# A memory-attention and two-layer MoE kernel: its first stage as 390 one-engine parts in a fixed order

## The chip, the cores and the metric

The kernel runs on one core of a Trainium2 chip. The metric is the device time of one execution in microseconds. The engines are TensorE (PE, with its weight loads as PEld), VectorE (DVE), ScalarE (ACT), GpSimd (POOL) and SyncE (SP), whose queue issues the loads and stores.

## The reference

Batch 4, 8 heads, 576 tokens, head size 64, 32 memory slots; the MoE layers have 512 to 1536 and back. The inputs are 64-bit floats; the kernel reads attention inputs as 32-bit floats and decodes weights from their two 32-bit halves.

```
a = exp(phi - max(phi, axis=2)); a = a / (sum(a, axis=2) + 1e-09)
k_m = einsum('bhsm,bhsd->bhmd', a, k)
v_m = einsum('bhsm,bhsd->bhmd', a, v)
scores = q @ k_m.T / sqrt(64)
attn = exp(scores - max); attn = attn / (sum(attn) + 1e-09)
x = (attn @ v_m), tokens by (heads x 64)
x = ((x @ w_a) * (x @ w_b)) @ w_out
g = x @ w_gate
out = (g * sigmoid(g) * (x @ w_val)) @ w_out2
```

## The kernel before

The work has three stages. The first is the attention of the four batches, together with the first two of the twelve column blocks (f = 0, 1) of the first MoE layer. The second stage is column blocks 2 to 11 of that layer, in five rounds of two. The third is the second layer. Matmuls that need more precision are made from a high and a low part: the high part is a ScalarE copy, the low part is the difference, on VectorE or GpSimd (`split`).

For each batch b the attention goes like this. `phi` is loaded; its maximum goes over the nine rows a partition holds (`over_r`, tiles `rm`, `pm`), then over partitions by TensorE (`mx`) and VectorE (`nmx`); `phi` is shifted and exponentiated. TensorE contracts it with k and v (`kv`, 144 instructions), its sum (`es`, on GpSimd) gives `rs`, which scales `kv` into `kvm`; TensorE transposes that (`kvT`) into `kb` and `vt`. `q` is transposed (`qT`). The scores come in two calls (`sc`, 40 instructions each: twice 16 and 4), each followed on VectorE by `mx`, a subtraction, ScalarE's exponential, `den` and a multiplication. The transposed result is `aT`, split high and low.

The first MoE layer never forms x @ w. `vw` is v_m times a weight block; `s1a` and `s1b` are the two products of `aT` with it (two products of 12 matmuls for each batch and block), `bs` their product, split into `gh` and `gl`; `s2` multiplies by `w_out` (`oh`, `ol`), in four parts of 12 matmuls for a batch and a pair of blocks, added into `acc`.

A weight chunk is 128 x 512. It is loaded (`raw`, four buffers, at most three chunks ahead), ScalarE and VectorE reshape its bits (`dec_a`, lines 123 to 134: three VectorE operations), GpSimd adds the two halves (lines 148, 150), and `w_out` chunks are split (172, 176). A chunk is 512 KB, a `phi` 576 KB, a half of k or v 576 KB, a `q` 1024 and 128 KB. All loads go through SyncE's queue in order. `q` of the last batch uses the slot of the third batch's transposed `q`, k and v of it use slots of batches 0 and 1.

The first stage is written by hand as a string, `PLAN`: a letter for a whole step of a batch (`0a`), `T` for the next weight chunk with all its operations, `V` for the next `vw` and `D` for the next step of `first_dense`. The framework's scheduler takes this order as a priority and issues each engine's instructions in an order of its own, by its estimates of time; it also mixes work of the second stage into the first. The first loads are in a string of their own, `LOADS`. The second and third stage have lists of their own (`BLOCK`, and the loops at the end).

All TensorE results go to `bank2` tiles: four buffers of two PSUM banks.

Of the kernel before, what the change touches and what calls it, by code (L numbers as in the profile page):

```python
# [18 lines left out]
def kernel(  # L19
# [75 lines left out]
    raw, dec, whl, ohl = {}, {}, {}, {}  # L95
# [24 lines left out]
    def chunk_bits(c):  # L120
        hi, lo = raw[c][:, :, 1], raw[c][:, :, 0]
        a = dec_p.tile([128, 512], I32, tag="a", name="dec_a")
        nc.scalar.activation(out=f32(a), in_=f32(hi), func=ACTF.Abs)
        nc.vector.tensor_scalar(  # L124
            out=f32(a), in0=f32(a), scalar1=LEAST, scalar2=MOST, op0=ALU.max, op1=ALU.min
        )
        nc.scalar.activation(  # L127
            out=lo, in_=lo.bitcast(U32), func=ACTF.Copy, scale=2.0 ** -29
        )
# [7 lines left out]
        dec[c] = a  # L137

    def chunk_round(c):
        a = dec.pop(c) if whole(c) else dec[c]  # L140
        lo = raw.pop(c)[:, :, 0]
        if whole(c):
            i, j = c
            if j == 0:
# [3 lines left out]
            nc.gpsimd.tensor_tensor(out=o, in0=ai, in1=li, op=ALU.add)  # L148
        else:
            nc.gpsimd.tensor_tensor(out=a, in0=a, in1=lo, op=ALU.add)  # L150

    def whole(c):

        return c[0] < NF and c[1] < 2

    def chunk_dst(c):
        i, j = c
        if j < 2:
            return [x[:, :, j, :] for x in whl[i]]
        return ohl[i]  # L160

    def chunk_src(c):
        a = f32(dec[c])
        return a.rearrange("p (k f) -> p k f", k=KD) if c[1] < 2 else a

    def chunk_hi(c):
        i, j = c
        if j == 0:
            whl[i] = [w_p.tile([128, KD, 2, 128], FP32R, tag="w", name=f"w{x}") for x in "hl"]
        elif j == 2:  # L170
            ohl[i] = [w_p.tile([128, DM], FP32R, tag=f"o{x}", name=f"o{x}") for x in "hl"]
# [9 lines left out]
    def ticks_to(n):  # L181
        while ticks[0] < n:
            t = ticks[0]
            for step in (chunk_bits, chunk_round, chunk_hi, chunk_lo):
                if step in (chunk_bits, chunk_round) or not whole(order[t]):
                    step(order[t])
# [49 lines left out]
    mx_t, et_t, kvm_t, qT_t, sc_t = {}, {}, {}, {}, {}  # L236
# [9 lines left out]
    def att_pre(b):  # L246

        m = at_p.tile([128, PR, M], FP32, tag="pm", name="pm")
        over_r(eng("rmx", b), m, phi_t[b], ALU.max)
        mx_t[b] = m  # L250

    def att_phi(b):

        pt = bank2("mx")
        nc.tensor.transpose(
            pt[:, 0, 0:128], mx_t.pop(b).rearrange("p j m -> p (j m)"), ident
        )
# [4 lines left out]
        )  # L262
        for g in range(2):
# [4 lines left out]
        m = pt[:, 1, 0:128]  # L268
        if eng("sub", b) is nc.gpsimd:
            m = at_p.tile([128, 128], FP32, tag="nm", bufs=1, name="nm")  # L270
            nc.scalar.copy(out=m, in_=pt[:, 1, 0:128])
        et_t[b] = m

    def att_norm(b):
        x = phi_t[b]
        m = et_t.pop(b).rearrange("p (j o m) -> p j o m", j=PR, o=1)
        eng("sub", b).tensor_tensor(
            out=x, in0=x, in1=m.to_broadcast([128, PR, R, M]), op=ALU.add
        )
        nc.scalar.activation(out=x, in_=x, func=ACTF.Exp)  # L280

    def att_kv(b):


        x = phi_t.pop(b)
        es = at_p.tile([128, PR, M], FP32, tag="es", bufs=1, name="es")
        over_r(eng("sum", b), es, x, ALU.add)
        pkv = bank2("kv")
        for r in range(R):
            for j in range(PR):  # L290
                for g in range(2):
# [8 lines left out]
                    )  # L300
        sm = pkv[:, 0, 2 * D:2 * D + 2]
        nc.tensor.matmul(
            sm, lhsT=es.rearrange("p j m -> p (j m)"), rhs=ones, start=True, stop=True
        )
        rs = sm_p.tile([128, 2], FP32, tag="rs", name="rs")
        nc.vector.tensor_scalar(out=rs, in0=sm, scalar1=1e-9, scalar2=None, op0=ALU.add)
        nc.vector.reciprocal(out=rs, in_=rs)
        kv = at_p.tile([128, 3, 2, D], FP32, tag="kvm", name="kvm")
        for g in range(2):
# [3 lines left out]
            )  # L313
            nc.vector.tensor_scalar(
# [3 lines left out]
        kvm_t[b] = kv  # L318
        if b + 2 < B:
            load_phi(b + 2)  # L320

    def att_blocks(b):


        kv = kvm_t.pop(b)
        pT = bank2("kvT")
        for i in range(3):
            nc.tensor.transpose(
                pT[:, 0, 128 * i:128 * i + 128], kv[:, i].rearrange("c o d -> c (o d)"), ident
            )  # L330
        kT = pT[:, 0, 0:256].rearrange("c (g j m) -> c g j m", g=2, j=PR)
        for o in range(2):
            rows = slice(D * o, D * o + D)
            nc.scalar.copy(out=kb[b % 2][rows, :, :, o], in_=kT[rows])
        nc.scalar.copy(out=vt[b], in_=pT[:, 0, 256:384])

    def att_q(b, c):


        if c == 0:  # L340
            qT_t[b] = slot(ld_slots[b][0], [128, PR * R // 2, 128], FP32, f"qT{b}")
            kv_t.pop((b, 0))
# [10 lines left out]
    def att_scores(b, t):  # L353

        if t == 0:
            sc_t[b] = at_p.tile([128, R, PR, M], FP32, tag="sc", name="sc")
        pc = bank2("sc")
        for o in range(2):
            j = 2 * t + o
            for r in range(0, R, 2):  # L360
                for g in range(2):
# [10 lines left out]
                    else:  # L372
# [31 lines left out]
    def att_out(b, c):  # L404

        if c == 0:
            aT[b] = slot(ld_slots[b][1], [128, 2, 2, S], FP32R, f"aT{b}")
            kv_t.pop((b, 1))
# [11 lines left out]
        split(  # L420
            dst[0], dst[1],
            pa[:, 0:n * 128].rearrange("c (r g p) -> c r g p", g=2, p=P),
        )

    def att_stage(b, s):

        {
            "a": lambda: att_pre(b), "b": lambda: att_phi(b), "c": lambda: att_norm(b),
            "d": lambda: att_kv(b), "e": lambda: att_blocks(b),
            "f": lambda: att_q(b, 0), "g": lambda: att_q(b, 1), "h": lambda: att_q(b, 2),  # L430
            "i": lambda: att_scores(b, 0), "j": lambda: att_scores(b, 1),
            "k": lambda: att_softmax(b, 0), "l": lambda: att_softmax(b, 1),
            "m": lambda: att_out(b, 0), "n": lambda: att_out(b, 1),
        }[s]()
# [215 lines left out]
    for _ in dense:  # L650
        pass
# [141 lines left out]
```

## Time and profile before

| | |
|---|---|
| median of 3 runs | 923.0 us (921.26 to 924.1) |
| profiled execution | 921.33 us, its span 919.5 us |
| TensorE (PE) busy | 861.4 us, 94% |
| VectorE (DVE) busy | 513.5 us, 56% |
| ScalarE (ACT) busy | 317.8 us, 35% |
| GpSimd (POOL) busy | 210.2 us, 23% |
| mean granted TensorE clock | 0.971 |

The span reaches from the first to the last instruction. A clock of 1.0 is TensorE's upper level, 2.4 GHz, 0.5 the lower, 1.2 GHz; a value between is a mean over a stretch. Busy matmuls overlap, so the durations of single ones add up to more than the time they take. In rows of the trace, L12 is a line of the kernel, "s" is the tile `s2` or `s4`, and PE matmuls in the trace count the passes of a 32-bit matmul one by one.

### The profile page before, as it was taken

The numbers are of one execution on the slowest core, as the hardware profiler recorded it, in microseconds if no ns is written. First come the engines' busy times: TensorE is split into PE (matmuls) and PEld (weight loads), VectorE is DVE, ScalarE is ACT, GpSimd is POOL, SyncE is SP. The second block draws the span as 40 slices with busy tenths as digits, with TensorE's granted clock in tenths as the row PEclk, the third lists the DMA queues.
The fourth block names the chain that finished last, engine by engine and source line by source line (L and its number), as shares of the span: only waits on it lengthen the run. The fifth ranks groups of instructions, "written<-read, shape, count | busy, mean of one in ns | idle before, by whom it ended". The sixth has DMA issues, their size and how long they took to land.

```text
span 919.5 us, 16206 instructions
## 1 busy us (share of the span) xinstructions
PE 861.4 (94%) x7068; PEld 799.8 (87%) x7068; DVE 513.5 (56%) x714; ACT 317.8 (35%) x502; POOL 210.2 (23%) x165
## 2 busy tenths in 40 slices
PE   3685897899999999999999999999999999999997
PEld 2574786789989989999999999999999999999995
DVE  3698637654765745649736316544554753644343
ACT  2465434542523424235424433312421420411210
POOL 2253013331422314315004203211220420410000
PEclk9687997999999999999999999999999999999999
DMA  9972104120211300202002201110210200000027
GB/s 330 375 240 92 53 3 138 47 92 1 92 47 47 112 4 24 70 1 92 1 1 69 70 1 46 46 47 1 92 47 1 91 25 1 1 1 1 1 46 160
DMA packets 42439, 60.02 MB, mean 65 GB/s; under 512 B 4224, under 2 KB 30848, under 8 KB 42368
## 3 DMA queue, kind: packets, MB, share of 16 engines
q1 hardware_dynamic: 42368, 58.99, 20.4%
q8 instruction: 55, 0.90, 0.4%
q14 instruction: 16, 0.13, 0.0%
HBM read 54.26 MB, written 4.72 MB: 64 GB/s over the span
## 4 chain that ended last, share of the span: by engine, by line
PE 71%; issue 10%; DVE 7%; DMA 6%; POOL 2%; SPq 2%; ACT 2%; POOLq 0%; ACTq 0%; DVEq 0%
PE s L460 27%; PE val L468 17%; PE gate L468 17%; PE s1b L468 5%; PE s1a L468 4%; DMA raw<-in_moe_w_b_dram 2%; DVE dec_a L124 2%; PE vw L481 2%; DMA q<-in_q_dram 2%; DVE dec_a L130 1%; DVE dec_a L134 1%; DMA raw<-in_moe_w_a_dram 1%; DMA raw<-in_moe_w_out_dram 1%; DVE gl L78 1%; DVE vwl L78 1%
## 5 line engine op out<-in xcount | busy, mean ns | idle before, releaser
L460 PE MATMUL s<-oh,g 128*128 128x512 f32 x432 | 137.0, 390 | 0.0
L460 PE MATMUL s<-gh,oh 128*128 128x288 f32 x384 | 114.6, 301 | 3.4 <-ACT gh L77 2.2
L460 PE MATMUL s<-gl,oh 128*128 128x288 f32 x384 | 113.2, 295 | 1.5 <-DVE gl L78 0.9
L460 PE MATMUL s<-gh,ol 128*128 128x288 f32 x384 | 112.9, 295 | 0.0
L698 DVE TENSOR_TENSOR sg<-gate,sg 128x576 f32<-128x576 f32 x48 | 36.3, 756 | 107.3 <-ACT sg L697 107.3
L460 PEld LDWEIGHTS s<-oh,g 128*128 128x128 f32 x432 | 81.1, 188 | 16.4
L176 POOL TENSOR_TENSOR wl<-dec_a,wh 128x512 fp32r<-128x512 f32 x24 | 36.3, 1536 | 250.4 <-ACT wh L172 244.7
L150 POOL TENSOR_TENSOR dec_a<-dec_a,raw 128x512 int32<-128x512 int32 x48 | 64.2, 1338 | 98.2 <-issue 44.2
L127 ACT ACTIVATE raw<-raw 128x512 int32<-128x512 uint32 x72 | 48.9, 680 | 107.4 <-DMA raw<-in_moe_w_out_dram 42.1
L460 PE MATMUL s<-ol,g 128*128 128x512 f32 x216 | 84.1, 389 | 0.0
L468 PE MATMUL gate<-x2l,wh 128*128 128x288 f32 x384 | 82.4, 296 | 0.0
L468 PE MATMUL val<-x2l,wh 128*128 128x288 f32 x384 | 82.2, 296 | 0.0
L468 PE MATMUL val<-x2h,wh 128*128 128x288 f32 x384 | 82.2, 296 | 0.0
L468 PE MATMUL val<-x2h,wl 128*128 128x288 f32 x384 | 82.2, 296 | 0.0
L559 DVE TENSOR_TENSOR acc<-s,acc 128x576 f32<-128x576 f32 x80 | 59.5, 751 | 40.5 <-PE s L460 40.4
L468 PE MATMUL gate<-x2h,wl 128*128 128x288 f32 x384 | 82.0, 295 | 0.0
L468 PE MATMUL gate<-x2h,wh 128*128 128x288 f32 x384 | 82.0, 295 | 0.0
L468 PE MATMUL s1b<-aT,vwh 128*128 128x288 f32 x384 | 75.8, 316 | 5.2 <-DVE aT L78 2.4
L460 PEld LDWEIGHTS s<-gh,oh 128*128 128x128 f32 x384 | 71.9, 188 | 6.6 <-ACT gh L77 3.0
L725 DVE TENSOR_TENSOR oacc<-s,oacc 128x1024 f32<-128x1024 f32 (+1 forms) x50 | 55.7, 1115 | 34.2 <-PE s L460 33.2
L460 PEld LDWEIGHTS s<-gl,oh 128*128 128x128 f32 x384 | 72.2, 188 | 2.0 <-DVE gl L78 1.2
L697 ACT ACTIVATE sg<-gate 128x576 f32<-128x576 f32 x48 | 31.2, 649 | 122.8 <-PE gate L468 122.8
(97 smaller groups left out, 1721.8 us busy)
## 6 DMA issues: line engine op xcount, KB each, us to landing
raw<-in_moe_w_out_dram SPq DMA_DIRECT2D x24, 512.0 KB, 3.4
raw<-in_moe_w_a_dram SPq DMA_DIRECT2D x12, 512.0 KB, 4.9
raw<-in_moe_w_b_dram SPq DMA_DIRECT2D x12, 512.0 KB, 3.6
raw<-in_moe_w_gate_dram SPq DMA_DIRECT2D x12, 512.0 KB, 3.5
raw<-in_moe_w_val_dram SPq DMA_DIRECT2D x12, 512.0 KB, 3.5
kv<-in_k_dram SPq DMA_DIRECT2D x8, 576.0 KB, 9.7
kv<-in_v_dram SPq DMA_DIRECT2D x8, 576.0 KB, 9.7
out_dram<-oacc SPq DMA_DIRECT2D x36, 128.0 KB, 2.4
```

The source lines that it names most:

```text
L78: (eng or nc.vector).tensor_tensor(out=lo, in0=src, in1=f32(hi), op=ALU.subtract)
L124: nc.vector.tensor_scalar(out=f32(a), in0=f32(a), scalar1=LEAST, scalar2=MOST, op0=ALU.max, op1=ALU.min)
L127: nc.scalar.activation(out=lo, in_=lo.bitcast(U32), func=ACTF.Copy, scale=2.0 ** -29)
L150: nc.gpsimd.tensor_tensor(out=a, in0=a, in1=lo, op=ALU.add)
L176: nc.gpsimd.tensor_tensor(out=lo, in0=chunk_src(c), in1=f32(hi), op=ALU.subtract)
L460: nc.tensor.matmul(dst, lhsT=l, rhs=r, start=(i == 0), stop=(i == n - 1))
L468: nc.tensor.matmul(p[:, hb, 0:HB], l, x, start=(i == 0), stop=(i == n - 1))
L481: nc.tensor.matmul(pv[M * j:M * j + M, g, n], lhsT=vt[b][rows, M * j:M * j + M], rhs=whl[f][0][rows, j].rearrange("p t c -> p (t c)"), sta ...
L559: nc.vector.tensor_tensor(out=acc[b][:, dt], in0=pv, in1=acc[b][:, dt], op=ALU.add)
L697: nc.scalar.activation(out=t, in_=pg, func=ACTF.Sigmoid)
L698: nc.vector.tensor_tensor(out=t, in0=pg, in1=t, op=ALU.mult)
L725: nc.vector.tensor_tensor(out=dst, in0=p[:, 0:n], in1=dst, op=ALU.add)
```

## The change

The steps of the first stage become generators that hand back after each group of instructions of one engine. `PLAN` becomes a list of 390 such parts: a name begins a piece of work when it first stands there, and each later time goes on to the next part of the same piece. `p` is `phi` to `kvT` and `kb` of a batch, `e` the sum, `q` the `qT`, `s` a score call with its softmax, `o` the `aT`, `a` and `b` the two products of `s1`, `d` a part of `s2`, `c` a weight chunk (by number), `v` a `vw`; capitals are loads (`P` phi, `K` and `L` halves of k and v, `Q` q, `W` a weight chunk). Afterwards each instruction of the list is tied behind the one before it on its engine, and each later instruction behind the engine's last of the list. These ties need no semaphore. The second and third stages' lists stay as they are.

```
-    def chunk_bits(c):
+    def chunk(c):
+        i, j = c
         hi, lo = raw[c][:, :, 1], raw[c][:, :, 0]
         a = dec_p.tile([128, 512], I32, tag="a", name="dec_a")
         nc.scalar.activation(out=f32(a), in_=f32(hi), func=ACTF.Abs)
+        yield
+        nc.scalar.activation(
+            out=lo, in_=lo.bitcast(U32), func=ACTF.Copy, scale=2.0 ** -29
+        )
+        yield
         nc.vector.tensor_scalar(
...
     PLAN = """
-    0a 0b 0c 0d T 1a 0f 0g 0e 0h 1b T 0i 1c 0k 0j 0l T 1d 0m T V 0n V 1e
...
+    P0 W1 L0 K0 W0 Q0 p0 P1 W3 c1 p0 c1 p0 p0 c1 K1 p0 c1 c1 c1 c1 p0 e0 L1 p0 Q1 c0 c0 c0 W2 c0
+    c0 c0 c0 p0 q0.1 p0 p0 q0.0 q0.1 W4 q0.2 q0.0 p0 p1 p0 q0.2 W5 c3 p0 p0 p0 p1 c3 s0.0 p1 c3
...
-    LOADS = "p0 k0 w0 l0 q0 w1 p1 w2 k1 l1 q1 k2 l2 q2"
...
+    begun = {}
     for op in PLAN.split():
...
+        if op not in begun:
+            begun[op] = work(op)
+        next(begun[op], None)
+    ticks[0] = sum(op[0] == "c" for op in begun)
+    n_vw[0] = sum(op[0] == "v" for op in begun)
...
+    def behind(ins, in_turn):
+        for x in ins:
+            if x.engine in engines and not isinstance(x, mybir.BassTilePoolBoundary):
+                if x.engine in last:
+                    tc.add_manual_dep(x, last[x.engine], no_sync, reason="order of the plan")
+                if in_turn:
+                    last[x.engine] = x.name
+
+    planned = list(nc.cur_bb.bb.instructions)
+    behind(planned, True)
...
     for _ in pend:
         pass
+    behind(list(nc.cur_bb.bb.instructions)[len(planned):], False)
```

Three pieces of the engines' orders follow, each before and then after. A row is a line of the program, the operation, and the tiles it writes and reads; numbers behind a name tell buffers apart.

The first piece is VectorE after the first batch's `phi` is shifted. Before, `rm` and `pm` are those of the second batch, `dec_a` rows belong to two weight chunks, and `rs` and `kvm` to the first batch:

```order
L241 TENSOR_TENSOR rm<-phi 128x384
L134 SCALAR_TENSOR_TENSOR dec_a<-raw,dec_a 128x512
L242 TENSOR_TENSOR rm<-rm,phi 128x384
L243 TENSOR_TENSOR rm<-rm 128x4x32
L244 TENSOR_TENSOR pm<-rm 128x128
L124 TENSOR_SCALAR dec_a<-dec_a 128x512
L130 TENSOR_SCALAR dec_a<-dec_a 128x512
L134 SCALAR_TENSOR_TENSOR dec_a<-raw,dec_a 128x512
L306 TENSOR_SCALAR rs<-kv 128x2
L307 RECIPROCAL rs<-rs 128x2
L314 TENSOR_SCALAR kvm<-kv,rs 128x64 x2
```

After, at the same place, the chunk is number 0:

```order
L134 TENSOR_SCALAR dec_a<-dec_a 128x512
L137 TENSOR_SCALAR dec_a<-dec_a 128x512
L141 SCALAR_TENSOR_TENSOR dec_a<-raw,dec_a 128x512
L287 TENSOR_SCALAR rs<-kv 128x2
L288 RECIPROCAL rs<-rs 128x2
L422 COPY qT_247<-qT 128x1024
L298 TENSOR_SCALAR kvm<-kv,rs 128x64 x2
L231 TENSOR_TENSOR rm<-phi 128x384
L232 TENSOR_TENSOR rm<-rm,phi 128x384
L233 TENSOR_TENSOR rm<-rm 128x4x32
```

The second batch's `rm` has moved from ahead of the first batch's `rs` to behind its `kvm`, and one chunk stands ahead of `rs` where parts of two stood.

The second piece is TensorE between `s2` and the next `s1`, in the middle of the stage. Before, `aT` is that of the third batch, the `s` rows are `s2` of the second, `kv` that of the fourth:

```order
L460 MATMUL s_1134<-gl,oh 128x288
L460 MATMUL s_1134<-gh,ol 128x288
L255 MATMUL mx<-ident,pm 128x128
L481 MATMUL vw<-w,vt_95 32x256 x16
L264 MATMUL mx<-ident,nmx 64x128 x2
L412 MATMUL aT<-ident,sc 128x128 x9
L468 MATMUL s1b<-aT_1190,vwh 128x288
L293 MATMUL kv<-kv_370,phi 32x128 x4
L293 MATMUL kv<-kv_723,phi 32x128 x4
```

After, `aT` and `s1b` are the second batch's; the `kv` sum just ended is the fourth's, `kvT` and the scores are the third's:

```order
L282 MATMUL kv<-ones,es 128x2
L307 MATMUL kvT<-ident,kvm 128x128 x3
L397 MATMUL aT<-ident,sc 128x128 x5
L350 MATMUL sc<-kb_97,qT_805 64x64 x8
L360 MATMUL sc<-kb_97,qT_805 64x32 x2
L350 MATMUL sc<-kb_97,qT_805 64x64 x8
L360 MATMUL sc<-kb_97,qT_805 64x32 x2
L350 MATMUL sc<-kb_97,qT_805 64x64 x8
L360 MATMUL sc<-kb_97,qT_805 64x32 x2
L350 MATMUL sc<-kb_97,qT_805 64x64 x8
L360 MATMUL sc<-kb_97,qT_805 64x32 x2
L435 MATMUL s1b<-aT_953,vwh 128x288 x4
```

Before, a batch's `aT` is followed by its own `s1`, and the next batch's scores come after that; now the next batch's scores stand between a batch's `aT` and its `s1`, and the batch after that has its `kv` done too.

The third piece is SyncE's queue around the last batch's `q`. Before, k and v of the last batch's second half, then `q`:

```order
L223 DMA kv_723<-in_k_dram 128x2x576
L223 DMA kv_723<-in_v_dram 128x2x576
L110 DMA raw<-in_moe_w_b_dram 128x4x256
L110 DMA raw<-in_moe_w_a_dram 128x4x256
L110 DMA raw<-in_moe_w_b_dram 128x4x256
L230 DMA q_1122<-in_q_dram 128x4x512
L230 DMA q_1122<-in_q_dram 128x4x64
```

After:

```order
L110 DMA raw<-in_moe_w_b_dram 128x4x256 x3
L213 DMA kv_756<-in_k_dram 128x2x576
L213 DMA kv_756<-in_v_dram 128x2x576
L110 DMA raw<-in_moe_w_a_dram 128x4x256 x2
L220 DMA q_1128<-in_q_dram 128x4x512
L220 DMA q_1128<-in_q_dram 128x4x64
L115 DMA raw<-in_moe_w_out_dram 128x1024
```

Three weight loads now stand ahead of the last batch's k and v, and two between them and `q`; two of these five chunks (12 and 13) belong to the second stage.

## Rows read from the trace of the kernel before

**Rows 1.** Windows: busy us of each engine (instructions), then PEclk, DMA share, GB/s.

```profile
0.00:200.00 200.00, 149.52 (x1845) 128.08 (x1846) 133.51 (x216) 93.87 (x159) 60.16 (x57) 0.87 0.47 157
84.00:147.00 63.00, 54.40 (x790) 46.84 (x789) 35.88 (x63) 23.96 (x44) 9.47 (x11) 0.93 0.11 33
200.00:459.10 259.10, 257.62 (x2279) 243.54 (x2279) 162.42 (x220) 100.69 (x155) 70.85 (x51) 1.00 0.14 44
```

**Rows 2.** Chain that ended last, second stage and start of third: start, us, what.

```profile
342.64 1.02 PE vw L481 x32
...
348.66 1.60 PE s1a L468 x12
...
459.11 3.20 PE gate L468 x24
```

**Rows 3.** Groups by line and shape, PE, 0 to 200 us: busy, mean ns, idle before.

```profile
L468 PE MATMUL s1b<-aT,vwh 128*128 128x288 f32 x104 | 25.2, 357 | 4.1 <-DVE aT L78 2.4 <-DVE bs L522 1.2 <-ACT aT L77 0.3
L460 PE MATMUL s<-gh,oh 128*128 128x288 f32 x76 | 23.2, 316 | 3.4 <-ACT gh L77 2.2 <-ACT acc L455 0.8 <-DVE vwl L78 0.4
...
L481 PE MATMUL vw<-w,vt 64*32 64x256 f32 x261 | 10.5, 414 | 1.8 <-POOL w L148 1.8
```

**Rows 4.** Timeline of DVE, first 26 us: start, us, what, idle before and releaser.

```profile
6.21 0.29 DVE L243 TENSOR_TENSOR rm<-rm 128x128 f32<-128x128 f32 x1
...
10.23 0.43 DVE L124 TENSOR_SCALAR dec_a<-dec_a 128x512 f32<-128x512 f32 x1 [0.33 <-ACT dec_a L123]
...
20.68 0.56 DVE L241 TENSOR_TENSOR rm<-phi 128x384 f32<-128x384 f32 x1 [1.68 <-DMA phi<-in_phi_dram]
...
22.34 1.27 DVE L243 TENSOR_TENSOR rm<-rm 128x128 f32<-128x128 f32 x1
...
25.38 0.15 DVE L306 TENSOR_SCALAR rs<-kv 128x2 f32<-128x2 f32 x1
```

**Rows 5.** Timeline of PE, 0 to 50 us, three starts after a wait.

```profile
26.24 0.47 PE L328 MATMUL kvT<-ident,kvm 128*128 128x128 f32 x1 [7.39 <-ACT kvm L310]
...
40.83 1.30 PE L412 MATMUL aT<-ident,sc 128*128 128x128 f32 x5 [2.20 <-DVE rs L306]
...
49.45 0.61 PE L468 MATMUL s1b<-aT,vwh 128*128 128x288 f32 x1 [1.14 <-DVE aT L78]
```

**Rows 6.** Groups by line and shape, DVE, 0 to 200 us.

```profile
L124 DVE TENSOR_SCALAR dec_a<-dec_a 128x512 f32<-128x512 f32 x25 | 20.2, 813 | 17.1 <-ACT dec_a L123 17.1
L134 DVE SCALAR_TENSOR_TENSOR dec_a<-raw,dec_a 128x512 int32<-128x512 int32 x25 | 20.2, 809 | 0.4
L130 DVE TENSOR_SCALAR dec_a<-dec_a 128x512 int32<-128x512 int32 x25 | 14.7, 589 | 0.3
L522 DVE TENSOR_TENSOR bs<-s1a,bs 128x576 f32<-128x576 f32 x12 | 9.0, 751 | 7.2 <-PE s1a L468 7.2
...
L78 DVE TENSOR_TENSOR vwl<-vw,vwh 128x1024 fp32r<-128x1024 f32 x4 | 4.9, 1220 | 4.8 <-ACT vwh L77 4.8
```

**Rows 7.** Timeline of PE, 90 to 109 us, full clock.

```profile
90.72 1.73 PE L293 MATMUL kv<-kv,phi 64*32 64x128 f32 x102
...
98.68 1.04 PE L347 MATMUL qT<-ident,q 128*128 128x128 f32 x8
...
106.54 0.69 PE L364 MATMUL sc<-kb,qT 128*64 128x64 f32 x16
...
108.01 0.30 PE L374 MATMUL sc<-kb,qT 64*64 64x32 f32 x4
```

**Rows 8.** Waits of PE, 0 to 300 us: total, times, longest.

```profile
PE aT L412 <- DVE sc L400: 17.4, 3, 8.8
```

**Rows 9.** Timeline of POOL at the held-up `rm`.

```profile
21.97 1.49 POOL L148 TENSOR_TENSOR w<-dec_a,raw 128x512 int32<-128x512 int32 x1 [5.82 <-DMA raw<-in_moe_w_a_dram]
```

**Rows 10.** Timeline of SP's queue: the last batch's `q`.

```profile
108.39 0.92 SPq L230 DMA_DIRECT2D q<-in_q_dram  x2
```

**Rows 11.** The tile `q`: its loads, issue to landing.

```profile
DMA to landing us min/median/max: 5.1/11.5/13.9
```

More of the change, by code (lines that the diff above doesn't have):

```diff
@@ L94 @@
     at = {c: n for n, c in enumerate(order)}
-    raw, dec, whl, ohl = {}, {}, {}, {}
+    raw, whl, ohl = {}, {}, {}
     def ready(i, j):
@@ L118, in chunk_load, with whole @@
         raw[c] = t
-    def chunk_bits(c):
+    def whole(c):
+        return c[0] < NF and c[1] < 2
+    def chunk(c):
+        i, j = c
         hi, lo = raw[c][:, :, 1], raw[c][:, :, 0]
@@ L183, in ticks_to @@
             t = ticks[0]
-            for step in (chunk_bits, chunk_round, chunk_hi, chunk_lo):
-                if step in (chunk_bits, chunk_round) or not whole(order[t]):
-                    step(order[t])
+            for _ in chunk(order[t]):
+                pass
             if t + AHEAD < len(order):
@@ L262, in att_phi @@
         )
+        yield
         for g in range(2):
@@ L267, in att_phi @@
             )
[L268 to L277, printed above, removed]
+        yield
+        m = pt[:, 1, 0:128].rearrange("p (j o m) -> p j o m", j=PR, o=1)
+        nc.vector.tensor_tensor(
             out=x, in0=x, in1=m.to_broadcast([128, PR, R, M]), op=ALU.add
         )
+        yield
         nc.scalar.activation(out=x, in_=x, func=ACTF.Exp)
[L282 to L287, printed above, removed]
+        yield
         pkv = bank2("kv")
@@ L313, in att_kv @@
             )
+        yield
+        for g in range(2):
             nc.vector.tensor_scalar(
@@ L520, in emit_s1, with s2_part @@
         yield
-        pa = prod(0, "s1a")
-        nc.vector.tensor_tensor(out=bs, in0=pa, in1=bs, op=ALU.mult)
+        nc.vector.tensor_tensor(out=bs, in0=pa_t.pop((b, f)), in1=bs, op=ALU.mult)
+        yield
+        vw_t.pop((b, f))
         g = [g_p.tile([128, 2, HB], FP32R, tag=f"g{x}", name=f"g{x}") for x in "hl"]
-        split(
-            g[0], g[1], bs,
-            eng("gl", 2 * b + f) if f < 2 else nc.gpsimd if f % 2 == 0 else nc.vector,
-        )
+        nc.scalar.copy(out=g[0], in_=bs)
+        yield
+        e = eng("gl", 2 * b + f) if f < 2 else nc.gpsimd if f % 2 == 0 else nc.vector
+        e.tensor_tensor(out=g[1], in0=bs, in1=f32(g[0]), op=ALU.subtract)
         g_t[b, f] = g
         yield
+    def emit_s1(b, f):
+        x = s1_b(b, f)
+        for n in range(2):
+            next(x)
+        yield
+        for _ in s1_a(b, f):
+            pass
+        for _ in x:
+            pass
+        yield
     acc, x2 = {}, {}
-    def emit_s2(b, idx):
+    def s2_part(b, idx, dt):
         first, last = idx[0] == 0, idx[-1] == NF - 1
-        if first:
+        if first and b not in acc:
             acc[b] = slot(ld_slots[b][2], [128, KD, 2, HB], FP32, f"acc{b}")
-        if last:
+        if last and b not in x2:
             x2[b] = [
@@ L634, with work @@
+    def work(op):
+        w, n = op[0], [int(x) for x in op[1:].split(".")]
+        return {
+            "p": att_phi, "e": att_sum, "q": att_q, "s": att_scores, "o": att_out,
+            "a": s1_a, "b": s1_b,
+            "c": lambda n: chunk(order[n]), "v": lambda n: vw_part(vws[n]),
+            "d": lambda b, dt: s2_part(b, (0, 1), dt),
+        }.get(w, lambda *n: load(w, *n))(*n)
     make_identity(nc, ident)
@@ L638 @@
         nc.vector.memset(ones[P * g:P * g + P, g:g + 1], 1.0)
-    dense = first_dense()
+    begun = {}
     for op in PLAN.split():
-        if op == "D":
-            next(dense, None)
-        elif op == "V":
-            next_vw()
-        elif op == "T":
-            ticks_to(min(ticks[0] + 1, before(4, 0)))
-        else:
-            att_stage(int(op[0]), op[1])
-    for _ in dense:
-        pass
+        if op not in begun:
[3 more added lines that the diff above has]
+    n_vw[0] = sum(op[0] == "v" for op in begun)
+    for b in range(B):
+        for f in range(2):
+            g_t.pop((b, f))
+    no_sync = mybir.DependencyInfo(
+        mybir.DependencyClass.NoSync, mybir.DependencyReason.DATA
+    )
+    engines = {e.engine for e in (nc.tensor, nc.vector, nc.scalar, nc.gpsimd, nc.sync)}
+    last = {}
+    def behind(ins, in_turn):
[7 more added lines that the diff above has]
+    behind(planned, True)
     s1, s2 = s1_parts(), s2_parts()
```

276 lines of the change are left out of this document (134 added, 142 removed).

## Prediction

> **What bounds the kernel now.** I read the windows first, because one number for the whole span hides everything here. From 200 us to 459.1 us TensorE is busy 257.62 of 259.10 us at full clock; in the first 200 us it is busy 149.52 us, and at a mean granted clock of 0.87 [rows 1]. So the second and third stages are bound by TensorE, the change doesn't touch their lists, and only the first stage has time to give.
>
> How much? I value what TensorE had done by 200 us at the prices of a full stretch: a product of 12 matmuls (`s1a`, `s1b`) takes 1.60 us, one part of `s2` is 12 matmuls of the same size, and a pair of `vw` parts takes 1.02 us [rows 2]. By 200 us it had issued 104 `vwh` matmuls of `s1b` (8 a product: 13 products, and the `s1a` that goes with each), 76 `gh,oh` matmuls of `s2` (4 a part: 19 parts) and 261 of `vw` (16 a part: 16.3 parts) [rows 3]. The first stage as the new list draws it needs 8, 8, 16 and 10 of these. The surplus is second-stage work: 10 products (16.0 us), 3 `s2` parts (4.8) and 6.3 `vw` parts (3.2), together 24.0 us. Without it the first stage would have ended at about 176 us.
>
> A second way to the same point: the first `gate` matmul starts at 459.11 [rows 2]. The second stage has five blocks, each of 16 products, 16 `s2` parts and 8 `vw` parts, 25.6 + 25.6 + 4.1 = 55.3 us; less the part `v8` that the list has already, 276 to 277 us in all. I allow 9 us for its own losses: about 6 is what separates 259.1 us after 200 from the 253 us of work then left, and 3 is an estimate for a ragged start. 459.1 - 277 - 9 = 173 us. I use this form below, since both kernels share it:
>
> span = T1 + 277 + 9 + (919.5 - 459.1 = 460.4), with T1 the end of the first stage on TensorE; before, T1 is 173.
>
> **What the change does, and its first milestone.** No arithmetic is added; the ties lie between instructions of one engine, which keeps its order anyway, so I cost them at nothing. What moves is which instruction an in-order engine has in front of it.
>
> Before, VectorE has the four `rm` operations of the second batch and two weight chunks ahead of `rs`. The first of these waits for its load until 20.68, `rs` runs at 25.38 [rows 4], and TensorE, done with `kv` early, idles 7.39 us before `kvT` at 26.24 [rows 5]. In the new order `rs` stands behind chunk 0 alone, and `rm` comes after `kvm` (first piece of the order above). The data for `kv` comes as before, since the same 3.5 MB are ahead of it. Chunk 0's load is the seventh instead of the eighth; with its three VectorE operations done by 17, `rs` is out at 17.2, one `qT` copy stands between, `kvm` is done at about 20.1, and `kvT` starts 6 us earlier than before.
>
> From `kvT` to the first `aT` transposes it took 40.83 - 26.24 = 14.6 us [rows 5]; the new order has one weight chunk and one `vwl` more in this chain, so I take 15.5 and get 35.6. From there to an unbroken `s1` before took 49.45 - 40.83 = 8.6 us [rows 5]. Now VectorE has `rs`, one chunk (0.81 + 0.59 + 0.81 = 2.2 us [rows 6]), `kvm` and both `aT` differences in front: 0.3 + 2.2 + 0.6 + 1.5 = 4.6 us. First `s1` at about 40.5, 9 us earlier.
>
> **The rest of the first stage.** TensorE's whole list at full clock: 16 products and 16 `s2` parts 51.2 us; 10 `vw` parts 5.1; 576 `kv` matmuls at 1.73/102 us, 9.8; 72 `qT`, 36 `aT` and 12 `kvT` transposes at 1.04/8 us, 15.6; 8 score calls at 108.31 - 106.54 = 1.77 us, 14.2 [rows 7]; some 3 us of small ones. Sum 99 us. Two batches of `kv` and scores, one and a half of `qT` and one `aT` are done at 40.5, 16 us; 83 are left, so TensorE can't end before 123.
>
> VectorE: 133.51 us busy in the first 200 us [rows 1]. Off that list are 13 of the 25 chunks (13 x 2.2 = 28.7), 4 of 12 `bs` (3.0), 3 of 4 wide `vwl` (3.7) [rows 6] and some five `acc` and `gl` of the same size as `bs` (3.8): 94.3 us are left. Adding up the new order's rows, some 25 of them are done at 35.6, so VectorE could end at 105, and behind its last difference TensorE has at most eight `s2` parts, 12.8 us: 118. The two engines are nearly level, so neither alone sets the end; handing over does.
>
> For that I use the middle batches before. From 84 to 147 us TensorE did two batches in 63 us, idle for 8.6 and at clock 0.93, worth 4.4 [rows 1]: 6.5 us lost for each batch, mostly in `aT` waiting for the softmax of its own batch, 17.4 us in three waits [rows 8]. The new order puts `s2` of the batch before, `kv` and scores of the next batch between those (second piece), so part of it is filled. Three batches are left: 19.5 us if nothing is filled, 0 if all is. I take 13, nearer the upper end, because an order that cannot move meets delays of its own and four two-bank PSUM tiles let TensorE run ahead little. T1 = 123 + 13 = 136.
>
> The loads cost nothing by this sum. Those of the third batch now stand behind a wait for the first batch's scores, which end at about 30 us in this walk, when the 12 MB asked for ahead of them are still landing until about 40: the loads up to the second `phi`, 5.8 MB, took until 20.68 [rows 4], 0.3 MB a us.
>
> Sum: 136 + 277 + 9 + 460.4 = 882.4 us of span, against 919.5. The profiled run took 921.33 us, 1.8 above its span, and the median of the runs shown is 1.7 above that. I predict **886 us**, 37 less.
>
> **Two rules of the Trainium skill.** An order that can't move pays for every late input with all that stands behind it; the row for that is VectorE's 1.68 us wait for a load at 20.68, with `rs` behind it, for which TensorE lost 7.39 [rows 4, 5]. The Trainium skill, "TensorE: Matmul & The Clock Gate", table of specifications, says that the queues of ScalarE, VectorE and GpSimdE are strict FIFO; the trace agrees. By that rule the change could as well make such waits as remove them, which is the slower rival's ground.
>
> A VectorE operation can also be held up by GpSimd: `rm` L243 takes 0.29 us at 6.21 with GpSimd idle and 1.27 us at 22.34, while GpSimd adds from 21.97 on [rows 4, 9]. The Trainium skill, "SBUF — State Buffer", section on the shared port pair, says this is an exclusive lock in which the loser fully blocks; the trace agrees, the long one ends just after GpSimd does. The rival it makes is worked out next.
>
> **Rivals.**
> *All handovers filled.* T1 = 123, span 869.4, time 873. For it: VectorE and TensorE are level and every batch has another's work beside it. Against: TensorE restarts at half clock at 40 us, and the losses never were zero in any batch before.
> *VectorE held up by GpSimd.* The first stage has some 38 us of GpSimd work (12 chunks at about 1.3 us, splits and sums), which now lies in 100 us instead of 170. The first operation of a chunk takes 0.43 us undisturbed, as at 10.23, and 0.81 in the mean [rows 4, 6]; if the other two lose as much together, 0.76 a chunk or 9 us of 12 chunks, about a quarter of GpSimd's time, is in my sum already. If all of it blocked, 28 us more fall on VectorE: 118 + 28 = 146, with half to all of the 13 us of handovers 152 to 159; time 902 to 909. Half as dense, it gives about 895.
> *Slower: the fourth batch's `q` comes late.* It is 1.1 MB that waits on the SyncE queue for the third batch's scores (their slot), and now also stands behind two weight loads that wait for GpSimd to free `raw` buffers (third piece). Before, it was issued at 108.39, and a `q` load takes 5.1 us at the least to land [rows 10, 11]. In my walk the scores end near 74 and those buffers come free at about the same time. What follows `qT` of the fourth batch is 45 us of TensorE, with some 8 of handovers, so T1 is the issue time + 58. From an issue at 118 us on, T1 is above 176 and the kernel slower; at 125 the time is about 933. For it: three waits in one queue; against: it needs a slip of over 40 us.
> *No change.* The old order was the scheduler's own, the new one moves the same work; if both wait for the same chains, T1 stays at about 173 and the time at 923. Against: TensorE lost over 70 of 200 us, and `rs` and `aT` show where.
>
> **Chances.** Forecast (876 to 895) 0.58; handovers filled (below 876) 0.12; VectorE held up (895 to 915) 0.20; no change 0.03; slower 0.07. The time is that of the first, 886. The range 870 to 906 takes in T1 from 123 to 156: most of the second case and three quarters of the third. About 0.3% (2.8 us) is what a measurement of this kernel tells from no change: faster 0.90, same 0.03, slower 0.07.
>
> **What would show it.** Right: `kvT` of the first batch near 20 us and the first `s1` near 41; TensorE's first second-stage product near 136; second stage and third as long as before (277 + 9 and 460); clock 1.0 from 50 us on. Wrong, and how: VectorE's chunk operations well over 2.2 us a chunk (held up); a TensorE wait for a `q` or `kv` load after 50 us (the loads' order); a T1 near 136 with a longer second stage, because it starts with 12 decoded chunks where before had 25 decoded at 200 us [rows 6]. That last one would break the sum at a place where I assumed that nothing changes.

## The result, and the profile after

The changed kernel took 885.63 us (median of 4 runs, 884.45 to 888.8), the kernel before 922.39 beside it: ratio 0.9605, 95% interval 0.9575 to 0.9636. The profiled execution took 884.45 us, span 882.7, mean granted clock 0.994 (before 0.971). 886 us were predicted, but that the sum came out is luck, through two errors of equal size: the first stage ended 14 us earlier than I put it, and the second stage took 14 us longer.

The windows show both. Columns as in [rows 1]; the cuts are the first unbroken `s1`, the end of the first stage (T1), 200 us, the first `gate`, and the last matmul.

```profile
0.00:40.50 40.50, 22.75 (x478) 18.36 (x479) 27.10 (x59) 19.13 (x34) 12.06 (x18) 1.00 1.01 348
40.50:122.30 81.80, 79.52 (x1120) 72.79 (x1126) 62.38 (x107) 46.91 (x82) 26.75 (x23) 1.00 0.41 135
122.30:200.00 77.70, 71.34 (x642) 65.63 (x643) 59.08 (x76) 38.19 (x60) 30.14 (x21) 0.96 0.28 88
200.00:422.20 222.20, 215.48 (x1890) 202.81 (x1890) 147.64 (x196) 90.89 (x139) 65.07 (x46) 1.00 0.15 49
422.20:876.40 454.20, 454.20 (x2953) 428.22 (x2951) 217.10 (x277) 123.30 (x188) 79.40 (x57) 1.00 0.12 36
```

In the second line TensorE (first busy column) is idle for 2.3 of 81.8 us at full clock, where before it lost 6.5 us a batch. In the third and fourth, the second stage, it is idle 6.4 and 6.7 us, 13 in all; before it was idle for 1.5 us from 200 us to the first `gate` [rows 1].

TensorE's timeline has the milestones. Columns: start, us, engine, line, operation, count, and in brackets the idle time before it and what ended it.

```profile
20.49 0.62 PE L307 MATMUL kvT<-ident,kvm 128*128 128x128 f32 x3 [0.31 <-DVE qT L422]
33.60 1.17 PE L397 MATMUL aT<-ident,sc 128*128 128x128 f32 x9 [0.43 <-DVE rs L287]
...
38.42 0.80 PE L435 MATMUL s1a<-aT,vwh 128*128 128x288 f32 x4
...
122.20 1.09 PE L448 MATMUL vw<-w,vt 64*32 64x256 f32 x32
...
142.23 0.61 PE L427 MATMUL s<-gh,oh 128*128 128x288 f32 x1 [4.31 <-DVE bs L493]
...
226.07 0.79 PE L435 MATMUL s1a<-aT,vwh 128*128 128x288 f32 x4 [1.48 <-DVE acc L543]
...
422.06 0.42 PE L435 MATMUL gate<-x2h,wh 128*128 128x288 f32 x2
```

The starts that answer to [rows 5] came at 20.5, 33.6 and 38.4 us. The `vw` at 122.20 stands right behind the last `s2` part of the first stage, so T1 is 122.2. The first `gate` is at 422.1: the second stage took 299.9 us. TensorE's three largest waits in it (total, times, longest):

```profile
PE s1a L435 <- DVE acc L543: 4.7, 4, 1.5
PE s L427 <- DVE bs L493: 4.3, 1, 4.3
PE s L427 <- DVE vwl L470: 2.0, 3, 1.1
```

One long stall stands at its start, at 142 us, after which TensorE ran at half clock (0.66 and 0.50 in the windows 140 to 144 and 144 to 148 us); four shorter ones, up to 1.5 us, stand at the turns of its rounds. VectorE is named in these rows; 2.0 us more fell to ScalarE (`gh`, `bs`). What VectorE did, by the groups of a weight chunk's three operations (count, busy, mean ns), first up to T1 and then from 122 to 171 us, where the second round begins:

```profile
L141 DVE SCALAR_TENSOR_TENSOR dec_a<-raw,dec_a 128x512 int32<-128x512 int32 x12 | 8.3, 693 | 0.4
L137 DVE TENSOR_SCALAR dec_a<-dec_a 128x512 int32<-128x512 int32 x12 | 6.2, 520 | 0.4
L134 DVE TENSOR_SCALAR dec_a<-dec_a 128x512 f32<-128x512 f32 x12 | 5.8, 487 | 4.5 <-ACT dec_a L128 4.5
...
L141 DVE SCALAR_TENSOR_TENSOR dec_a<-raw,dec_a 128x512 int32<-128x512 int32 x13 | 11.5, 895 | 0.1
L137 DVE TENSOR_SCALAR dec_a<-dec_a 128x512 int32<-128x512 int32 x13 | 11.2, 869 | 0.2
L134 DVE TENSOR_SCALAR dec_a<-dec_a 128x512 f32<-128x512 f32 x13 | 9.9, 766 | 8.4 <-ACT dec_a L128 8.4
```

Twelve chunks took 1.70 us each in the first 122 us; then 13 chunks crowd into 49 us and take 2.53 us each. VectorE's timeline just ahead of the long stall, and the same stretch of GpSimd's:

```profile
134.95 1.53 DVE L134 TENSOR_SCALAR dec_a<-dec_a 128x512 f32<-128x512 f32 x1
136.52 1.55 DVE L137 TENSOR_SCALAR dec_a<-dec_a 128x512 int32<-128x512 int32 x1
138.10 1.65 DVE L141 SCALAR_TENSOR_TENSOR dec_a<-raw,dec_a 128x512 int32<-128x512 int32 x1
139.68 0.41 DVE L134 TENSOR_SCALAR dec_a<-dec_a 128x512 f32<-128x512 f32 x1
140.12 1.38 DVE L137 TENSOR_SCALAR dec_a<-dec_a 128x512 int32<-128x512 int32 x1
141.43 0.74 DVE L493 TENSOR_TENSOR bs<-s1a,bs 128x576 f32<-128x576 f32 x1
```

```profile
134.51 1.69 POOL L151 TENSOR_TENSOR w<-dec_a,raw 128x512 int32<-128x512 int32 x1 [0.96 <-DVE dec_a L141]
136.15 1.62 POOL L500 TENSOR_TENSOR gl<-bs,gh 128x576 fp32r<-128x576 f32 x1
137.75 1.46 POOL L153 TENSOR_TENSOR dec_a<-dec_a,raw 128x512 int32<-128x512 int32 x1
```

The `bs` that TensorE needs stands behind five decode operations. While GpSimd works on one thing after another, the first three of them take 1.5 to 1.7 us; the fourth, with GpSimd idle, takes 0.41, and the same three operations took 0.43, 0.43 and 0.69 at 123.6 us, when GpSimd was idle too.

### The profile page after: what moved, and what is told of

Its sections match the earlier page's. It is cut to its first block, busy times and chain, and to the rows that moved or that the text cites. A ratio compares the mean times of both kernels' runs of the same rounds, so it can differ in the third digit from the quotient of the medians.

```text
span 882.7 us, 16199 instructions
## 1 busy us (share of the span) xinstructions
PE 843.4 (96%) x7068; PEld 787.8 (89%) x7068; DVE 514.0 (58%) x714; ACT 318.4 (36%) x502; POOL 213.4 (24%) x165
## 4 chain that ended last, share of the span: by engine, by line
PE 79%; DVE 9%; DMA 4%; issue 3%; ACT 2%; SPq 1%; POOL 1%; ACTq 0%; POOLq 0%
PE s L427 29%; PE val L435 17%; PE gate L435 17%; PE s1b L435 6%; PE s1a L435 5%; PE vw L448 2%; DVE dec_a L141 2%; DVE dec_a L134 2%; DVE dec_a L137 1%; DMA raw<-in_moe_w_b_dram 1%; DVE acc L543 1%; PE sc L350 1%; DMA phi<-in_phi_dram 1%; DMA raw<-in_moe_w_gate_dram 1%; DVE bs L493 1%
## 5 line engine op out<-in xcount | busy, mean ns | idle before, releaser
L745 DVE TENSOR_TENSOR oacc<-s,oacc 128x1024 f32<-128x1024 f32 (+1 forms) x50 | 55.7, 1115 | 34.6 <-PE s L427 33.6
L717 ACT ACTIVATE sg<-gate 128x576 f32<-128x576 f32 x48 | 31.1, 648 | 122.3 <-PE gate L435 122.1
L427 PEld LDWEIGHTS s<-gh,ol 128*128 128x128 f32 x384 | 72.6, 189 | 0.0
```

The lines of the kernel that those rows point to most:

```text
L427: nc.tensor.matmul(dst, lhsT=l, rhs=r, start=(i == 0), stop=(i == n - 1))
L717: nc.scalar.activation(out=t, in_=pg, func=ACTF.Sigmoid)
L745: nc.vector.tensor_tensor(out=dst, in0=p[:, 0:n], in1=dst, op=ALU.add)
```

## The experiments

Eleven kernels. For each, T1, the first `gate`, the second stage's length between them, and the time; the kernel before ran beside each of the three groups and gave 921.96, 922.16 and 922.11 us. Stage times are those of the one profiled execution; T1 is the end of the last `s2` part of the list. The changed kernel, e8, e8b, e9, e10 and e11 have the same tied list, so where their T1 differ, the edit is not the cause; the last section shows what is.

| kernel | T1 | first `gate` | second stage | time, us | ratio to before, 95% |
|---|---|---|---|---|---|
| changed | 122.2 | 422.1 | 299.9 | 885.63 | 0.9575 to 0.9636 |
| e1 rest untied | 141.8 | 435.1 | 293.3 | 897.68 | 0.9715 to 0.9761 |
| e2 chunks in the list | 132.1 | 431.3 | 299.2 | 889.97 | 0.9609 to 0.9692 |
| e3 list, no ties | 154.2 | 445.2 | 291.0 | 909.37 | 0.9838 to 0.9890 |
| e4 old order, tied | 183.9 | 478.4 | 294.5 | 938.42 | 1.0157 to 1.0206 |
| e5 first piece undone | 129.1 | 430.0 | 300.9 | 891.92 | 0.9658 to 0.9700 |
| e7 `q` late | 138.4 | 439.7 | 301.3 | 901.77 | 0.9750 to 0.9797 |
| e8 held back | 122.1 | 424.6 | 302.5 | 888.35 | 0.9617 to 0.9659 |
| e8b held back, later | 127.1 | 429.9 | 302.8 | 891.35 | 0.9647 to 0.9683 |
| e10 `gl` on VectorE | 125.9 | 424.0 | 298.1 | 885.67 | 0.9588 to 0.9619 |
| e9 six chunks a block | 127.3 | 417.6 | 290.3 | 875.18 | 0.9485 to 0.9533 |
| e11 e9 and e10 | 121.5 | 405.9 | 284.4 | 872.32 | 0.9448 to 0.9486 |

**What in the change carries it.** e1 takes the ties off everything behind the list, e3 off the list too, and e4 ties the order that the kernel before was written in.

```diff
 e1 and e3:
-    behind(list(nc.cur_bb.bb.instructions)[len(planned):], False)
 e3 as well:
-    behind(planned, True)
 e4, in the kernel before: the function behind(), and these two calls at the same places
```

> The list stays tied; the second and third stages are no longer tied behind it. Debt theory: the tie keeps ScalarE from weight chunks 12 to 14 until its last acc copy at 122.31 us, VectorE idles 5.37 and 6.86 us before that, and the second stage pays for it with a late start. Untied, chunks are decoded from about 106 us on; the first stage still ends on TensorE at 122 to 125, the second takes 286 to 291 us instead of 300, time 872 to 878. Order theory: the second stage's 23 us over its 277 lie in the scheduler's order of it, round after round; nothing moves, 883 to 888.

> The new list as a mere priority: both sets of ties are gone. Theory that the list carries the gain: the scheduler's estimates lead to nearly the same orders, first stage ends at 122 to 130, time 872 to 890. Theory that the tie carries it: the scheduler moves second-stage work and weight chunks ahead of attention as before, first stage's own work is done at 145 to 170, time 895 to 915.

> The kernel before with its old coarse plan, each engine tied to the order in which that plan writes its instructions, the rest tied behind. If ties by themselves gave the gain: 885 to 905. If it is the fine list: every step of a batch runs end to end on its engines and nothing fills the waits, first stage 190 to 240 us long, time 940 to 990.

e1 missed both expectations: slower by 12 us, all of it and more in T1, which is 19.6 us later. Rows of the longest wait show how it begins; ScalarE's, then TensorE's timeline of e1.

```profile
41.81 0.65 ACT L130 ACTIVATE raw<-raw 128x512 int32<-128x512 uint32 x1 [6.76 <-DMA raw<-in_moe_w_a_dram]
42.37 0.61 ACT L292 ACTIVATE kvm<-kv,rs 128x128 f32<-128x128 f32 x2
```

```profile
43.63 1.94 PE L332 MATMUL qT<-ident,q 128*128 128x128 f32 x8 [7.52 <-DVE kvm L298]
```

With the later work free to move, the scheduler put an operation of chunk 14, which belongs to the second stage, ahead of the second batch's `kvm` on ScalarE. On the chip its load landed late, and `kvm`, and TensorE, waited 7 us behind it; the granted clock was then 0.70 from 40 to 60 us, against 1.00 in the changed kernel. The rest of the 19.6 us is not broken down here. So this tie is not about order inside the list; it keeps later work out of it.

e3 came as the theory of the ties said. Without them the old pattern is back: VectorE's `rm` waits for its load ahead of `rs`, just as in [rows 4].

```profile
19.53 0.56 DVE L231 TENSOR_TENSOR rm<-phi 128x384 f32<-128x384 f32 x1 [2.71 <-DMA phi<-in_phi_dram]
...
24.33 0.15 DVE L287 TENSOR_SCALAR rs<-kv 128x2 f32<-128x2 f32 x1
```

e4 landed just below the range expected if the fine list is needed (its T1 is approximate, since its stages overlap): ties alone cost 1.8%. The list alone gains 1.4%, both together 4.0%; neither is the change without the other.

**Do delays in the first stage carry through?** e5 moves the second batch's `rm` and `pm`, with three parts of chunk 3, ahead of `rs` again. e7 puts the last `q` load behind one weight load more (and a part of chunk 8, for whose buffer that load waits, a little earlier).

```diff
 e5
-    c0 c0 c0 p0 q0.1 p0 p0 q0.0 q0.1 W4 q0.2 q0.0 p0 p1 p0 q0.2 W5 c3 p0 p0 p0 p1 c3 s0.0 p1 c3
+    c0 c0 c0 p0 q0.1 p1 c3 c3 c3 p0 p0 q0.0 q0.1 W4 q0.2 q0.0 p0 p0 q0.2 W5 p0 p0 p0 p1 s0.0 p1
 e7
-    b1.0 Q3 s2.0 c8 ... b1.1 c8 q3.0 b1.1 q3.2 c8 c8 c8 c8 q3.1 q3.0 s2.1 v5 q3.2 q3.1 W10
+    b1.0 s2.0 c8 ... b1.1 c8 c8 W10 Q3 q3.0 b1.1 q3.2 c8 c8 c8 q3.1 q3.0 s2.1 v5 q3.2 q3.1
```

> The changed kernel with the first piece of the order undone: the second batch's `rm`/`pm` and chunk 3's first parts stand ahead of `rs` of the first batch again, on VectorE. The prediction's walk (the first milestone carries through): `kvT` 3 to 5 us later than 20.5, first `s1` and the end of the first stage as much later, 888 to 891. Rival (later work has room): `kvT` late, but made up by 122 us: 884 to 887.

> The changed kernel with the fourth batch's `q` load placed behind one weight load more on SyncE's queue, right ahead of its own first `qT` part (in the changed kernel it was issued at 72.4 us and its transposes began at 80.3). The prediction's formula, end of the first stage = issue + 58 (or + 50, since no handover was lost), gives 133 to 141 for an issue near 83, and 895 to 903. With the data some 5 us after the issue the transposes would begin near 88, 8 us late: if that carries through as the first milestone did, the end is at 128 to 131 and the time 891 to 894. Rival (absorbed: the second batch's products fill the gap, as TensorE had no handover losses): 884 to 887.

In e5 `kvT` waits again (TensorE's timeline) and starts 5.2 us later; the first `s1` starts 7.4 us later, at a clock of 0.76 and 0.73 in the two stretches of 10 us from 20 us on (1.00 in the changed kernel). T1 is 6.9 and the time, by the medians, 6.3 us later: carried through, none of it absorbed.

```profile
25.66 0.87 PE L307 MATMUL kvT<-ident,kvm 128*128 128x128 f32 x3 [5.66 <-DVE qT L422]
```

In e7 the weight load held SyncE's queue longer than I thought, and `q` was issued at 88.64 us instead of 72.41 (timeline of SyncE's queue); the transposes waited for it (TensorE's timeline).

```profile
88.64 0.94 SPq L220 DMA_DIRECT2D q<-in_q_dram  x2
```

```profile
95.02 3.61 PE L332 MATMUL qT<-ident,q 128*128 128x128 f32 x18 [8.64 <-DMA q<-in_q_dram]
```

T1 is 138.4, issue + 49.8, which is 16.2 us up; the time is 16.1 us up. The rule with + 50 fits, and + 58 would have given 146.6. That it fits to tenths is partly luck: the transposes began 6.4 us after the issue, 1.5 less than in the changed kernel, and behind the long wait the clock was 0.81 for 8 us (window below), which costs 1.5.

```profile
95.00:103.00 8.00, 7.98 (x103) 7.08 (x104) 4.30 (x8) 3.51 (x6) 0.00 (x0) 0.81 0.01 2
```

**Where the second stage's 14 us went.** The first idea was a debt: the second stage starts with too little decoded. e2 puts three chunks more into the list's tail, where VectorE idles. e8 and e8b keep the decode of the first block from standing ahead of `bs`.

```diff
 e2
-    c11 c11 b3.1 d2.1 d2.0 b3.1 b3.1 d2.2 b3.1 d2.0 b3.1 d3.0 d2.2
+    c11 c11 c12 c12 c12 c12 W15 b3.1 d2.1 d2.0 b3.1 c13 c13 c13 c13 W16 b3.1 d2.2 b3.1 d2.0 b3.1
+    c14 c14 c14 c14 W17 d3.0 d2.2
 e8, in ticks_to; hold[0] is the last `bs` of this block
+            if hold[0]:
+                x = next(x for x in nc.cur_bb.bb.instructions[m:] if x.engine == nc.vector.engine)
+                tc.add_manual_dep(x, hold[0], no_sync, reason="behind bs")
 e8b as well, in the loop over BLOCK; n counts its words
+        if op == "T" and n < 30:
+            continue
```

> Everything stays tied, but weight chunks 12, 13, 14 and the loads 15, 16, 17 are put into the list ahead of the last s2 parts. Debt theory: some 6 us of VectorE work move from after 123 us into its idle stretch before; the 4.3 us wait at 142 and the half clock after it shrink or go; first stage ends at 122 to 124, time 876 to 881. Order theory: the same as the changed kernel, 884 to 887.

> The changed kernel with one tie more in the first block of the second stage: the first VectorE operation of each weight chunk that this block asks for may not stand ahead of the last `bs` written before it in the block. (The scheduler had put nine chunks' operations ahead of the third `bs`, though the block's products need none of them before about 170 us.) Theory run-ahead: TensorE's 4.3 us stall at 142 us and the half clock after it come from those decode operations standing in front of `bs` on VectorE; the stall goes or shrinks to 1 to 2 us, the clock holds, 3 to 7 us less: 878 to 883. Theory debt: the same VectorE work has to be done before the block's end, so the wait only moves to a `vw` or `s2` a little later: 884 to 889.

> As the run before, and the first nine chunks that the first block asks for are dropped from its first 30 words, so that VectorE has only `bs`, `gl`, `vwl` and `acc` until about 145 us. Run-ahead theory: no stall at all at the start, 6 to 8 us less than the changed kernel, 877 to 880. Debt theory: the decode of the second block's weights then falls into 150 to 175 us, `vw` or `acc` waits there, and the time is 884 to 892.

e2 gained nothing (its T1 is late partly because the clock fell, 0.64 from 20 to 30 us): its second stage took as long (299.2), with a 4.13 us wait for `bs` at the same distance from T1. VectorE decoded ten chunks in the 49 us behind T1 instead of 13, still four more than the next block needs, and the stall stayed. e8 and e8b came out by the debt theory, if for another reason, as the next run showed: the stall at 142 us is gone, and the loss moved. Windows of e8, which answer to 51.6 us of TensorE in the same two of the changed kernel:

```profile
122.00:145.00 23.00, 22.73 (x212) 20.62 (x211) 16.47 (x22) 14.99 (x24) 8.91 (x6) 1.00 0.19 55
145.00:180.00 35.00, 27.84 (x231) 24.38 (x230) 31.14 (x42) 17.14 (x27) 17.14 (x12) 0.95 0.47 146
```

That is 50.6 us: moving the decode inside the stretch changes nothing. But must there be so much of it? A round uses up six chunks; the block's list asks for 17, and the scheduler takes all whose buffers are free. e9 keeps the tie of e8 in all rounds and lets each block ask for six. e10 moves every `gl` from GpSimd to VectorE, e11 does both.

```diff
 e9
-            ticks_to(min(ticks[0] + 1, len(order)))
+            ticks_to(max(ticks[0], min(ticks[0] + 1, 18 + 6 * (n // 53))))
 e10 and e11
-        e = eng("gl", 2 * b + f) if f < 2 else nc.gpsimd if f % 2 == 0 else nc.vector
+        e = eng("gl", 2 * b + f) if f < 2 else nc.vector
```

> The changed kernel with every `gl` difference of the second stage on VectorE (in before and after those of even f are on GpSimd). Theory port: at each turn of a round the decode operations on VectorE are held up beside GpSimd's `gl` (1.66 and 1.94 us instead of 0.4 and 0.7), so three `acc` updates come late and `s1a` waits 1.1 to 1.5 us, four times; without GpSimd there the waits go, 4 to 6 us less, 880 to 882. Theory load: VectorE gets 20 operations of 0.75 us more, its `acc` come as late as before: 884 to 889.

> The changed kernel with the weight decode of the second stage paced: each of its five blocks decodes only the six chunks that the next block needs (18 - 12, and so on), and a chunk's first VectorE operation may not stand ahead of the last `bs` written before it. So far some 13 chunks were decoded between 122 and 165 us, with VectorE full, although the next block needs six of them, at about 171. Theory run-ahead (VectorE is full there only because it decodes two blocks ahead, since the scheduler takes what is ready): the 11 us lost after the first stage shrink to 2 to 4, and with no decode at a turn of a round the waits of `s1a` for `acc` go too; first `gate` at 405 to 413, time 868 to 876. Theory debt (the decode in that stretch is work that has to be done then, as the two holding runs suggest): first `gate` at 420 or later, time 883 to 890.

> As the run before, and every `gl` of the second stage on VectorE, so that GpSimd has only the chunks' sums and splits. Run-ahead theory with the port: 1 to 3 us below the run before. Debt theory: above it, VectorE has 20 operations of 0.75 us more.

e9 took 9.6 us off the second stage and, by the medians, 10 off the time: run-ahead it was. Its first `gate` (417.6) is later than expected only because T1 was (below). But e9 makes two changes, so here is the second stage in two parts, its first 49 us and the rest, for the changed kernel and then e9 (windows):

```profile
122.20:171.20 49.00, 42.64 (x363) 39.58 (x363) 45.00 (x58) 29.57 (x49) 25.98 (x18) 0.93 0.41 130
171.20:422.10 250.90, 244.18 (x2169) 228.85 (x2169) 161.71 (x213) 99.47 (x151) 69.23 (x49) 1.00 0.14 45
```

```profile
127.30:176.30 49.00, 46.24 (x427) 41.92 (x427) 31.53 (x41) 26.17 (x41) 17.11 (x12) 1.00 0.21 66
176.30:417.60 241.30, 237.47 (x2105) 223.84 (x2104) 164.47 (x226) 100.92 (x153) 81.89 (x55) 1.00 0.19 56
```

In the first part TensorE's idle time falls from 6.4 to 2.8 us, and with the clock back at 1.00 some 3 us of half clock are gone. There the tie alone, in e8, had left 6.7 us idle, so this is the smaller number of chunks. In the rest idle time falls from 6.7 to 3.8 us; there the tie is new as well as the number, and no run separates the two.

e10 alone is the same as the changed kernel: the waits of `s1a` for `acc` at the turns are gone and TensorE's idle time in the stage falls from 13.1 to 9.2 us, but the time isn't shorter, so neither theory's figure is shown. On top of e9, though, the same edit shortens the second stage by 5.9 us more in the one profile of each. The medians are 2.9 us apart and the executions overlap (e9 874.73 to 879.96, e11 868.25 to 875.26), so the size of this gain is not settled. Second stages of e9 and e11 (windows; GpSimd is the last engine):

```profile
127.30:417.60 290.30, 283.72 (x2530) 265.77 (x2530) 196.00 (x267) 127.09 (x194) 99.00 (x67) 1.00 0.19 57
```

```profile
121.50:405.90 284.40, 282.48 (x2530) 265.68 (x2530) 195.79 (x287) 127.46 (x193) 68.53 (x47) 1.00 0.19 59
```

VectorE has 20 operations more in e11 and is busy no longer, because its others are held up less. The last of a chunk's three, from 122 to 171 us, in e9 and then e11:

```profile
L141 DVE SCALAR_TENSOR_TENSOR dec_a<-raw,dec_a 128x512 int32<-128x512 int32 x6 | 6.3, 1062 | 0.0
```

```profile
L141 DVE SCALAR_TENSOR_TENSOR dec_a<-raw,dec_a 128x512 int32<-128x512 int32 x6 | 4.4, 740 | 0.0
```

The Trainium skill, "SBUF — State Buffer", section "SBUF: two separate sides", says that a VectorE operation with two inputs in SBUF, as this one has, and a GpSimd operation that reads SBUF take a shared port pair as a lock for a whole instruction; these rows agree, with 1062 ns beside more GpSimd work and 740 beside less. e11, at 872.32 us, has the lowest median found: 13 us below the changed kernel by the medians, each beside the same kernel before.

## Why the prediction was right, and where it wasn't

**Bound and form of the sum: right.** The third stage took 882.7 - 422.1 = 460.6 us (460.4 taken), and e5 and e7 show that a delay of T1 comes out in the time one to one.

**First milestone: right.** `kvT` at 20.5 (20.1), first `aT` at 33.6 (35.6), unbroken `s1` at 38.4 (40.5). The 0.9 us allowed for a chunk more in the chain was not needed. One name was off: the load that stood eighth before was chunk 1's, and chunk 0's was the fourth. Nothing hung on it, since chunk 0 was done at 16.9 and `rs`, at 17.86, came behind a wait for `kv`. e5 shows that the move of `rs` is the cause.

**TensorE's floor: right.** 83 us of work were left by the sum; TensorE took 83.8 from 38.4 us to T1, idle for 2 to 3. VectorE's floor of 118 lay below it, as said; VectorE was busy for 89.5 us up to T1, where the sum had 94.3.

**Handovers, 13 us: wrong.** They cost next to nothing, so T1 was 122.2 and not 136. This is the rival "all handovers filled" (T1 = 123), which I gave 0.12. The restart at half clock at 40 us that I held against it did not come in this profile: the clock was 1.00 up to T1. I took two thirds of the loss before as given, arguing that an order that can't move meets delays of its own. e5 and e7 show that such delays do carry through, but the list leaves few to meet; e3 and e4 show what they cost where it doesn't.

**Second stage's losses, 9 us: wrong, they were 23.** 299.9 - 277: 13.1 idle, some 3 at half clock (0.96 over 77.7 us), and about 7 that count as busy, near the 6 in the prediction. The 277 was itself 1 to 2 us high: five blocks of 55.3 us less the 1.02 of `v8` are 275.4. The 9 were taken from the same figure, so 277 + 9 hardly moves. The prediction named this as the place where the sum could break, but with the wrong cause. Starting from 12 decoded chunks isn't it: e11 starts from the same 12 and needs 284.4 us, 1.6 less than the 286 I had, and three chunks more (e2) gained nothing. What e9 shows is that decode beyond the needs of the next round stood in front of the products. Why the kernel before didn't pay for its run-ahead is argued, not shown: its first stage, slow on TensorE, left VectorE time for it, and 19 chunks were decoded by 173 us, the T1 that the prediction gives it.

**VectorE held up by GpSimd: right in kind, wrong in place.** Not in the first stage, where a chunk took 1.70 us against 2.2 before, but behind it, at 2.53. The operation's mean in e11 against e9 shows it, and e10 that taking `gl` from GpSimd isn't enough alone. The 38 us of GpSimd work in the first stage were right (38.8), and the forecast that they would hold VectorE up there was not.

**Late `q`: the rule was right but for its handovers, the case didn't come.** The issue was at 72.41 (74 in the walk), and the transposes at 80.31 followed without a gap, so nothing waited for `q`. The test is e7, where TensorE did wait: the distance to T1 was 50 us there, the 8 us of handovers in it again being too many.

**Chip time for ties and loads, nothing: right for the loads,** TensorE waited for none after 50 us. No run prices the ties by themselves, and that was the wrong question: without them the list is worth a third (e3).

What stays open: e10 alone removes waits at the turns without a shorter time. Its list is the changed kernel's, so its T1, 3.7 us later in the profiled execution, is not the edit's doing: the clock was 0.66 from 20 to 30 us there and 1.00 in the changed kernel. Whether its 1.8 us gain in the second stage is real, the medians (885.67 and 885.63) can't tell.

## What to carry to other kernels

Work that an engine can do ahead in a slow stage doesn't vanish when the stage gets faster, and it may then stand in front of what the next stage needs: look for the engine that runs ahead, and cut the work back to what is needed by then. Here six chunks a round instead of all that fit, tied behind the products, gave 10 us. An order that is tied needs to be fine enough that no engine stands behind another's load, and a fine order needs ties on what comes after it too, or the scheduler slips later work in between.

## Unexpected of the hardware

The first stage is tied, so e9 and e11 have the same instructions in the same order there, yet T1 was 127.3 and 121.5. The clock differs: windows 20 to 40 and 60 to 80 us, of e9 and then e11.

```profile
20.00:40.00 20.00, 15.52 (x299) 12.01 (x299) 17.06 (x37) 12.46 (x24) 5.49 (x6) 0.83 1.07 379
60.00:80.00 20.00, 18.04 (x288) 16.35 (x289) 14.38 (x27) 9.39 (x21) 6.12 (x6) 0.74 0.33 103
```

```profile
20.00:40.00 20.00, 14.51 (x309) 11.38 (x310) 18.18 (x40) 13.38 (x26) 5.91 (x6) 1.00 1.06 379
60.00:80.00 20.00, 18.32 (x345) 16.32 (x344) 17.11 (x31) 11.85 (x26) 5.45 (x6) 1.00 0.37 114
```

TensorE is idle for 4.5 and 5.5 us in the first stretch and for 2.0 and 1.7 in the second, much alike, and the clock falls to its lower level, 1.2 GHz, for a part of them in one and not in the other. The same list goes both ways in the other kernels that have it: T1 is 122.2 and 122.1 in the changed kernel and e8, at clock 1.00 from 20 to 40 us, and 127.1 and 125.9 in e8b and e10, where it fell. That is worth some 4 to 6 us of a stage of 122, so a single profile doesn't tell T1 closer than that. It is why medians carry the comparisons of times above, and the stage lengths, from one profile each, only go beside them.
